# Retention attention and a Snake MLP in one kernel: state sums on VectorE, separate PSUM banks, and a lagged product

## The chip, the cores and the metric

The kernel runs on 1 core of one Trainium2 chip. The metric is device time in microseconds (us). The core has TensorE (PE; its weight loads are shown apart as PEld), VectorE (DVE), ScalarE (ACT), GpSimd (POOL) and SyncE (SP, which here only issues DMAs). Each engine works through its own instructions in order and waits for others by semaphores.

## What is computed

Eight batches of causal attention without softmax, each with 8 heads, 576 tokens and 64 dimensions, with a decay per head; the outputs of all heads are laid side by side and go through an MLP (512 to 2048 to 512) with the Snake activation:

```python
scores = scale * (q @ k.T)                     # per batch and head
ret    = scores * gamma[h] ** (i - j)          # for j <= i, else 0
x      = ret @ v                               # 4608 tokens x 512
h      = x @ w_in
g      = h + sin(alpha * h) ** 2 / (alpha + 1e-9)
out    = g @ w_out
```

## The kernel before, in words

**Attention.** The decay is folded into q and k: `cast` (L121) multiplies the float32 rows by a factor per token and writes float16. A batch has 576 tokens, taken as part 0 (tokens 0 to 255), part 1 (256 to 511) and a small part 2 (the last 64). A part has two chunks of 128 tokens, 0 and 1, or 2 and 3. For each part:

- `transposes` (L155) turns k and q on PE into PSUM (`tr`); `take` (L183) copies them to SBUF (`T`).
- `scores` (L232) multiplies them, in two calls (y = 0, 1) of two head groups each, and masks the result on DVE into `ret`. `scores_small` (L256) does it for part 2. "Mask (p, y)" below is this DVE instruction.
- `outer` (L192) forms the sum of k times v of each chunk (`kv` in PSUM) and copies it on ACT to SBUF (`kvs`). With `spare=True` it uses two banks of the tag `hp`, else two of `mm`.
- `chain` (L218) on POOL: sum n becomes sum n plus the decayed sum n-1 (L223, L224), and the state n, two decayed copies in float16, is made from it (L225).
- `values` (L275) multiplies `ret` with v; `add_states` (L296) adds the part that comes from earlier chunks through the states (part 0 needs state 0, part 1 states 1 and 2, part 2 state 3), and one ACT copy puts the result into `xT` (L311, L316), the input of the MLP.

**The MLP** takes blocks of 512 tokens, nine in all. `gemm1` (L325) computes one of 16 units of a block (128 columns of the hidden layer, 4 matmuls of 128x512) and issues the Sin on ACT; `square` (L341) squares it on a given engine; `product` (L350) on DVE adds the square over alpha to the PSUM value and writes `gT`. Only `product` gives a unit's PSUM bank free. `gemm2` (L361) multiplies `gT` with `w_out` in 16 units, four per output tile; after each fourth one, ACT copies the tile out (`osb`) and SP stores it.

**PSUM** has eight banks: the tag `mm` has two buffers of two banks (transposes, scores, values), `hp` three of one, `op` one. A buffer is waited for until all that used it before is done.

**Order.** Nothing is scheduled automatically: the order in which the code issues instructions is the order on each engine (L384 on). First comes the attention of batch 0, parts 0 and 1, one step after the other (L395 to L426), then alpha's transposition (L427 to L431). The weights come through POOL's DMA queue: `load_w_in` in two halves, `load_w_out` in four groups. On SP, the small DMA `gate` (L434) reads a piece of w_out and so holds the loads behind it back until that group has landed. Then:

- Block 0 (L438 to L446), software-pipelined by hand: gemm1 of unit u, square of u-1 (DVE, ACT and POOL in turn), product of u-2. Units 1 and 2 of every four share one two-bank `mm` tile, `wide`; the others take `hp`.
- gemm2 of block 0, units 0 to 11 (L465), with part 2 of batch 0 and parts 0 and 1 of batch 1 hung on its units by the table `todo` (L450).
- The rest of batch 1's part 1 (L469 to L476).
- Blocks 1 to 8 (L479 on): per unit gemm1 of block n, attention steps of a later batch by the table `todo`, square, product, and gemm2 of block n-1. In block 1 the squares of odd units are on ACT, and the rest of gemm2 of block 0 is done.

Of the kernel before, what the change touches and what calls it, by code (L numbers as in the profile page):

```python
# [9 lines left out]
F32 = mybir.dt.float32  # L10
F16 = mybir.dt.float16
ADD = mybir.AluOpType.add
# [4 lines left out]
def kernel(  # L17
# [128 lines left out]
    class Attention:  # L146
        def __init__(self, b):
            self.b = b
            self.c0 = b * S
            self.T = {}  # L150
            self.ret = {}
            self.state = work.tile([P, 4, 4, 2, D], F16, tag="s16", bufs=2, name="s16")
            self.kvs = work.tile([P, 4, 4, D], F32, tag="kvs", bufs=1, name="kvs")

# [37 lines left out]
        def outer(self, ps, spare=False):  # L192
            if spare:
                kv = [psum.tile([P, 512], F32, tag="hp", bufs=3, name="kv") for g in range(2)]
            else:
                kv2 = psum.tile([P, 2, 512], F32, tag="mm", bufs=2, name="kv")
                kv = [kv2[:, g] for g in range(2)]
            todo = [(x, a, r) for x in range(len(ps)) for a in range(4) for r in range(2)]
            for n, (x, a, r) in enumerate(todo):
                for t in range(2):  # L200
                    for g in range(2):
                        nc.tensor.matmul(  # L202
                            kv[g][halves(t), 256 * x + 64 * a : 256 * x + 64 * a + 64],
                            half[self.b, "k", ps[x]][halves(g), head_of(a, t), r, :],
                            half[self.b, "v", ps[x]][halves(g), head_of(a, t), r, :],
                            start=(n == 0), stop=(n == len(todo) - 1), skip_group_check=True,
                        )
            N = len(ps)
            if spare:
                for g in range(2):  # L210
                    nc.scalar.copy(self.kvs[:, 2 * ps[0] + g], kv[g][:, 0:256].rearrange("p (a d) -> p a d", a=4))
            else:
                nc.scalar.copy(  # L213
                    self.kvs[:, 2 * ps[0] : 2 * ps[0] + 2 * N].rearrange("p (x g) a d -> p g x (a d)", g=2),
                    kv2[:, :, 0 : 256 * N].rearrange("p g (x y) -> p g x y", x=N),
                )

        def chain(self, chunks):  # L218
            kvs = self.kvs
            for n in chunks:  # L220
                if n > 0:
                    s32 = work.tile([P, 4, D], F32, tag="s32", bufs=2, name="s32")
                    nc.gpsimd.tensor_tensor(s32, kvs[:, n - 1], g1.unsqueeze(2).to_broadcast([P, 4, D]), MULT)  # L223
                    nc.gpsimd.tensor_tensor(kvs[:, n], s32, kvs[:, n], ADD)  # L224
                nc.gpsimd.tensor_tensor(  # L225
                    self.state[:, n],
                    kvs[:, n].unsqueeze(2).to_broadcast([P, 4, 2, D]),
                    g2.unsqueeze(3).to_broadcast([P, 4, 2, D]),
                    MULT,
                )  # L230

        def scores(self, p, y):  # L232
            sc = psum.tile([P, 2, 512], F32, tag="mm", bufs=2, name="sc")
            T = self.T[p]
            for z in range(2):
                a = 2 * y + z
                for r in range(2):
                    for t in range(2):
                        for g in range(2):
                            x = 256 * z + 128 * r  # L240
                            nc.tensor.matmul(  # L241
                                sc[halves(g), t, x : x + 128],
                                T[halves(t), g, 0, 128 * a + 64 * r : 128 * a + 64 * r + 64],
                                T[halves(t), g, 1, 128 * a : 128 * a + 128],
                                start=(z == 0 and r == 0), stop=(z == 1 and r == 1), skip_group_check=True,
                            )
            ret = work.tile([P, 2, 512], F16, tag="ret", bufs=4, name="ret")
            nc.vector.tensor_tensor(  # L248
                ret.rearrange("p t (z x) -> p (t z) x", z=2),
                sc.rearrange("p t (z x) -> p (t z) x", z=2),  # L250
                mask[:, 0:256].unsqueeze(1).to_broadcast([P, 4, 256]),
                MULT,
            )
            self.ret[p, y] = ret
# [70 lines left out]
    def gemm1(n, fc, o=None):  # L325
# [4 lines left out]
        for a in range(KT):  # L330
# [1 line left out]
                hps, w_in16[:, a, fc * P : (fc + 1) * P], xT[:, a, bs0 : bs0 + 512],  # L332
                start=(a == 0), stop=(a == KT - 1),
            )
        s_t = work.tile([P, 512], F16, tag="s", bufs=3, name="s_t")
        nc.scalar.activation(  # L336
            s_t, hps, mybir.ActivationFunctionType.Sin, bias=0.0, scale=alpha_t[:, fc : fc + 1],
        )
# [1 line left out]

    def square(n, fc, eng):  # L341
        hps, s_t = hps_of[n, fc]
        ss_t = work.tile([P, 512], F16, tag="ss", bufs=3, name="ss_t")
        if eng is nc.scalar:
            nc.scalar.activation(ss_t, s_t, mybir.ActivationFunctionType.Square)  # L345
        else:
# [36 lines left out]

    with tc.manual_schedule():  # L384
        nc.scalar.dma_start(cn, cn_dram.ap())
        loads(0, (0, 1))
        nc.scalar.dma_start(ident, ident_dram.ap())
        nc.scalar.dma_start(mask, mask_dram.ap())
        nc.scalar.dma_start(alpha_r, moe_alpha.rearrange("(a p) -> a p", p=P))
# [6 lines left out]
        cast(0, "k", 0, V)  # L396
        A.transposes(0, "k")
        A.take(0, "k", A_)
        cast(0, "q", 0, V)
        A.transposes(0, "q")  # L400
        A.take(0, "q", A_)
        cast(0, "v", 0, G_)
        load_w_in(0)
        A.scores(0, 0)
        A.outer((0,), spare=True)
        A.chain((0, 1))
        load_w_in(1)
        cast(0, "k", 1, V)
        A.scores(0, 1)
        A.transposes(1, "k")  # L410
        A.take(1, "k", A_)
        cast(0, "q", 1, V)
        A.transposes(1, "q")
        cast(0, "v", 1, A_)
        A.take(1, "q", A_)
        A.values(0)
        A.add_states(0)
        A.outer((1,), spare=True)
        A.chain((2,))
        for g in range(4):  # L420
            load_w_out(g)
        A.chain((3,))
        A.scores(1, 0)
        A.scores(1, 1)
        A.values(1)
        A.add_states(1)  # L426
        al_ps = psum.tile([P, FC], F32, tag="hp", bufs=3, name="al_ps")  # L427
        nc.tensor.matmul(al_ps, alpha_r, eye, start=True, stop=True, is_transpose=True)
        nc.scalar.copy(alpha_t, al_ps)
        nc.vector.tensor_scalar_add(inva, al_ps, 1e-9)  # L430
        nc.vector.reciprocal(inva, inva)  # L431
# [17 lines left out]
        todo = {  # L449
            0: [lambda: cast(0, "k", 2, V), lambda: cast(0, "q", 2, V), lambda: cast(0, "v", 2, G_)],  # L450
            2: [lambda: cast(1, "k", 0, V)],
            3: [lambda: A.transposes(0, "k"), lambda: A.take(0, "k", A_), lambda: cast(1, "q", 0, V),
                lambda: loads(1, (2,))],
            4: [lambda: A0.transposes(2), lambda: A0.take(2, "k", V), lambda: A0.take(2, "q", V)],
            5: [lambda: A.transposes(0, "q"), lambda: A.take(0, "q", A_), lambda: cast(1, "v", 0, G_),
                lambda: load(2, "k", 0)],
            6: [lambda: A0.scores_small(), lambda: cast(1, "k", 1, V)],
            7: [lambda: A.scores(0, 0), lambda: A.outer((0,)), lambda: A.chain((0, 1)), lambda: load(2, "q", 0)],
            8: [lambda: A.scores(0, 1), lambda: cast(1, "q", 1, V), lambda: load(2, "v", 0)],
            9: [lambda: A0.values(2), lambda: A0.add_states(2)],  # L460
            10: [lambda: A.transposes(1), lambda: A.take(1, "k", A_), lambda: cast(1, "v", 1, A_),
                 lambda: A.take(1, "q", A_), lambda: load(2, "k", 1)],
            11: [lambda: A.values(0), lambda: A.add_states(0), lambda: load(2, "q", 1)],
        }
        for u in range(12):  # L465
            gemm2(0, u, "hp")
# [113 lines left out]
```

## Time and profile before

| | us |
|---|---|
| median of 3 runs | 347.95 (347.75 to 348.88) |
| the profiled execution | 347.28 |
| its span (first to last instruction) | 345.5 |
| PE busy | 311.0 (90%) |
| DVE busy | 243.6 (71%) |
| ACT busy | 180.4 (52%) |
| POOL busy | 152.7 (44%) |
| first gemm1 of block 0 | at 25.57 |
| first gemm1 of block 1 | at 70.32 |

A profile line of the timeline gives the start, the duration, the engine, the source line, the operation with its tiles and shapes, and in brackets how long the engine idled before and what released it. Busy times overlap between engines; a busy PE is not PE at its peak. PEclk is the granted TensorE clock: 1.00 is full.

### The profile page before, as it was taken

How to read it: one execution, taken by the hardware profiler on the slowest of the kernel's cores; microseconds unless marked ns; L12 is line 12 of the kernel's file. 1: busy time of each engine (PE TensorE's matmuls, PEld its weight loads, DVE VectorE, ACT ScalarE, POOL GpSimd, SP SyncE). 2: the span in 40 equal slices, each digit the busy share in tenths (PEclk: the TensorE clock that was granted, in tenths of full speed). 3: DMA queues.
4: the chain of work that ended last, by engine and by line, in shares of the span. 5: the costliest groups of instructions: out<-in, count | busy, mean ns of one | idle time of the engine just before them, and what ended most of it. 6: DMA issues, size and time to landing. Idle time of an engine off the chain costs nothing.

```text
span 345.5 us, 9540 instructions
## 1 busy us (share of the span) xinstructions
PE 311.0 (90%) x4097; PEld 152.5 (44%) x4097; DVE 243.6 (71%) x345; ACT 180.4 (52%) x268; POOL 152.7 (44%) x155
## 2 busy tenths in 40 slices
PE   0378879688899999999999999999999999999994
PEld 0253334434444454445454445544454444444441
DVE  2734686549889998899589858985895666666600
ACT  2345733567685555555555656555555445444511
POOL 0994323565596994598069707960810000000000
PEclk9999999879999999999999999999999999999998
DMA  8999697968724931982298129712111111211142
GB/s 212 256 146 200 122 299 209 236 160 243 163 45 120 251 101 30 260 200 49 46 265 193 35 62 267 194 34 46 33 33 30 32 31 30 58 35 30 31 89 65
DMA packets 72683, 42.72 MB, mean 124 GB/s; under 512 B 15664, under 2 KB 67008, under 8 KB 72640
## 3 DMA queue, kind: packets, MB, share of 16 engines
q1 hardware_dynamic: 68880, 37.78, 44.2%
q0 software_dynamic: 3264, 4.20, 7.4%
q8 instruction: 32, 0.52, 0.6%
q10 hardware_dynamic: 496, 0.13, 0.2%
q14 instruction: 11, 0.09, 0.1%
HBM read 36.83 MB, written 9.44 MB: 134 GB/s over the span
## 4 chain that ended last, share of the span: by engine, by line
PE 75%; DVE 11%; ACT 6%; POOL 3%; issue 2%; DMA 2%; SPq 0%; ACTq 0%; POOLq 0%; DVEq 0%
PE ops L367 32%; PE hps L331 32%; DVE ret L248 3%; PE tr L178 3%; PE o L303 2%; PE o L291 2%; PE sc L241 2%; DVE gT L352 2%; DVE k L133 2%; ACT T L188 2%; DMA q<-in_q_dram 2%; DVE ss_t L347 1%; ACT s_t L336 1%; PE kv L202 1%; DVE q L133 1%
## 5 line engine op out<-in xcount | busy, mean ns | idle before, releaser
L336 ACT ACTIVATE s_t<-hps,alpha_t 128x512 f16<-128x512 f32 x144 | 98.7, 687 | 109.8 <-PE hps L331 108.1
L331 PE MATMUL hps<-xT,w_in 128*128 128x512 f16 x576 | 149.1, 386 | 7.3 <-ACT s_t L336 3.5
L367 PE MATMUL ops<-w_out,gT 128*128 128x512 f16 x576 | 145.1, 380 | 0.0
L352 DVE SCALAR_TENSOR_TENSOR gT<-ss_t,inva,hps 128x512 f16<-128x512 f16 x144 | 107.1, 747 | 11.9 <-ACT ss_t L345 6.7
L347 DVE TENSOR_TENSOR ss_t<-s_t 128x512 f16<-128x512 f16 x126 | 77.0, 611 | 37.6 <-ACT s_t L336 37.5
L331 PEld LDWEIGHTS <-w_in 128*128 128x128 f16 x576 | 56.5, 99 | 76.1 <-issue 12.8
L367 PEld LDWEIGHTS <-gT 128*128 128x128 f16 x576 | 52.7, 98 | 58.2 <-DVE gT L352 0.3
L225 POOL TENSOR_TENSOR s<-kvs,cn 128x512 f16<-128x512 f32 x32 | 36.3, 1135 | 66.1 <-ACT kvs L213 64.2
L248 DVE TENSOR_TENSOR ret<-sc,mask 128x1024 f16<-128x1024 f32 x32 | 38.1, 1218 | 12.5 <-PE sc L241 12.5
L373 ACT COPY osb<-ops 128x512 f32<-128x512 f32 x36 | 21.1, 586 | 19.1 <-PE ops L367 17.4
L188 ACT COPY T<-tr 128x1024 f16<-128x1024 f16 (+1 forms) x28 | 23.1, 829 | 15.0 <-PE tr L178 13.6
L133 POOL TENSOR_TENSOR q<-q,cn 128x1024 f16<-128x1024 f32 x12 | 23.9, 1988 | 0.0
L224 POOL TENSOR_TENSOR kvs<-s,kvs 128x256 f32<-128x256 f32 x24 | 17.4, 724 | 9.6 <-ACT kvs L213 4.1
L311 ACT CAST xT<-o 128x1024 f16<-128x1024 f32 x16 | 16.2, 1014 | 9.9 <-PE o L303 9.9
L133 POOL TENSOR_TENSOR k<-k,cn 128x1024 f16<-128x1024 f32 x10 | 20.2, 2023 | 0.0
L137 POOL CAST v<-v 128x1024 f16<-128x1024 f32 x12 | 14.4, 1197 | 10.8 <-DMA v<-in_v_dram 10.8
L190 DVE COPY T<-tr 128x1024 f16<-128x1024 f16 (+1 forms) x20 | 10.5, 529 | 11.7 <-ACT T L188 11.0
L178 PE MATMUL tr<-ident,k 64*64 64x64 f16 x512 | 7.5, 201 | 11.9 <-DVE k L133 11.9
L223 POOL TENSOR_TENSOR s<-kvs,cn 128x256 f32<-128x256 f32 x24 | 18.0, 752 | 0.0
L241 PE MATMUL sc<-T 64*64 64x128 f16 x512 | 12.3, 230 | 4.5 <-ACT T L188 2.2
L241 PEld LDWEIGHTS <-T 64*64 64x64 f16 x512 | 9.3, 113 | 10.9 <-issue 10.7
L178 PEld LDWEIGHTS <-k 64*64 64x64 f16 x512 | 5.7, 114 | 18.0 <-DVE k L133 12.5
(45 smaller groups left out, 151.0 us busy)
## 6 DMA issues: line engine op xcount, KB each, us to landing
out_dram<-osb SPq DMA_DIRECT2D x72, 128.0 KB, 2.3
k<-in_k_dram SPq DMA_DIRECT2D x16, 512.0 KB, 5.1
q<-in_q_dram SPq DMA_DIRECT2D x16, 512.0 KB, 5.8
v<-in_v_dram SPq DMA_DIRECT2D x16, 512.0 KB, 6.8
w_in<-in_moe_w_in_dram POOLq DMA_DIRECT2D x8, 256.0 KB, 7.0
w_out<-in_moe_w_out_dram POOLq DMA_DIRECT2D x4, 512.0 KB, 10.2
ks<-in_k_dram SPq DMA_DIRECT2D x16, 64.0 KB, 3.8
qs<-in_q_dram SPq DMA_DIRECT2D x16, 64.0 KB, 3.4
```

Of the source, the lines that this page charges most:

```text
L133: eng.tensor_tensor(d_, s_, f_, MULT)
L178: nc.tensor.matmul(tr[halves(t), g, col : col + 64], x_, ident[halves(g), :], start=(n == 0), stop=(n == len(todo) - 1), is_transpose=True ...
L188: eng.copy(self.T[p][:, :, w, :], s_)
L225: nc.gpsimd.tensor_tensor(self.state[:, n], kvs[:, n].unsqueeze(2).to_broadcast([P, 4, 2, D]), g2.unsqueeze(3).to_broadcast([P, 4, 2, D]), ...
L241: nc.tensor.matmul(sc[halves(g), t, x : x + 128], T[halves(t), g, 0, 128 * a + 64 * r : 128 * a + 64 * r + 64], T[halves(t), g, 1, 128 * a ...
L248: nc.vector.tensor_tensor(ret.rearrange("p t (z x) -> p (t z) x", z=2), sc.rearrange("p t (z x) -> p (t z) x", z=2), mask[:, 0:256].unsque ...
L331: nc.tensor.matmul(hps, w_in16[:, a, fc * P : (fc + 1) * P], xT[:, a, bs0 : bs0 + 512], start=(a == 0), stop=(a == KT - 1),)
L336: nc.scalar.activation(s_t, hps, mybir.ActivationFunctionType.Sin, bias=0.0, scale=alpha_t[:, fc : fc + 1],)
L347: eng.tensor_tensor(ss_t, s_t, s_t, MULT)
L352: nc.vector.scalar_tensor_tensor(gT[n][:, fc, :], ss_t, inva[:, fc : fc + 1], hps, MULT, ADD)
L367: nc.tensor.matmul(o, gT[n][:, fk, c * P : (c + 1) * P], w_out16[:, fk, :], start=(fk == 0), stop=(fk == FC - 1),)
L373: nc.scalar.copy(osb, o)
```

## The change

- Each unit of block 0 gets a bank of its own out of six: even units `hp`, odd ones in turn one half of an `mm` buffer, another, and `op`.
- In batch 0, and in part 1 of batch 1, the chunk sums aren't copied to SBUF and added by POOL. `sum_in_place` copies only sum 0 on ACT and adds the others on DVE, straight from PSUM, in four instructions of 128x64 per chunk; POOL keeps the states (`to_state`).
- `scores` is split into its PE part and its mask, so that a cast can go between them.
- alpha's transposition moves up between the transposes of k and q; the loads of batch 0's last 64 tokens go right behind its other loads; the gate waits for w_out group 1 instead of 2; the second half of w_in is issued behind the states 0 and 1.
- Part 2 of batch 0 moves from gemm2 of block 0 into block 0; the table `todo` of gemm2 is rearranged accordingly, with values (0) at unit 10.
- The squares of block 0 are shared out anew (7 on DVE, 6 on ACT, 3 on POOL; before 6, 5 and 5), and the buffers `s` and `ss` go from 3 to 4.
- In block 1 the product lags by one unit: it is issued behind the next unit's square, and the last one in block 2.

```diff
             if spare:
-                for g in range(2):
-                    nc.scalar.copy(self.kvs[:, 2 * ps[0] + g], kv[g][:, 0:256].rearrange("p (a d) -> p a d", a=4))
+                self.kv = kv
...
+        def sum_in_place(self, p):
+            kv = [self.kv[g][:, 0:256].rearrange("p (a d) -> p a d", a=4) for g in range(2)]
+            if p == 0:
+                nc.scalar.copy(self.kvs[:, 0], kv[0])
+            for c in range(max(1, 2 * p), 2 * p + 2):
+                for a in range(4):
+                    nc.vector.scalar_tensor_tensor(
+                        self.kvs[:, c, a], self.kvs[:, c - 1, a], g1[:, a : a + 1], kv[c % 2][:, a], MULT, ADD
+                    )
+
+        def to_state(self, n):
+            nc.gpsimd.tensor_tensor(
+                self.state[:, n],
+                self.kvs[:, n].unsqueeze(2).to_broadcast([P, 4, 2, D]),
+                g2.unsqueeze(3).to_broadcast([P, 4, 2, D]),
+                MULT,
+            )
...
-        s_t = work.tile([P, 512], F16, tag="s", bufs=3, name="s_t")
+        s_t = work.tile([P, 512], F16, tag="s", bufs=4, name="s_t")
...
-        ss_t = work.tile([P, 512], F16, tag="ss", bufs=3, name="ss_t")
+        ss_t = work.tile([P, 512], F16, tag="ss", bufs=4, name="ss_t")
...
-        loads(0, (0, 1))
+        loads(0, (0, 1, 2))
...
         A.take(0, "k", A_)
+        al_ps = psum.tile([P, FC], F32, tag="hp", bufs=3, name="al_ps")
+        nc.tensor.matmul(al_ps, alpha_r, eye, start=True, stop=True, is_transpose=True)
         cast(0, "q", 0, V)
         A.transposes(0, "q")
         A.take(0, "q", A_)
+        nc.scalar.copy(alpha_t, al_ps)
+        nc.vector.tensor_scalar_add(inva, al_ps, 1e-9)
+        nc.vector.reciprocal(inva, inva)
         cast(0, "v", 0, G_)
         load_w_in(0)
-        A.scores(0, 0)
+        A.scores_pe(0, 0)
+        cast(0, "k", 1, V)
+        A.scores_mask(0, 0)
         A.outer((0,), spare=True)
-        A.chain((0, 1))
-        load_w_in(1)
-        cast(0, "k", 1, V)
-        A.scores(0, 1)
+        A.scores_pe(0, 1)
         A.transposes(1, "k")
         A.take(1, "k", A_)
         cast(0, "q", 1, V)
+        A.sum_in_place(0)
+        A.to_state(0)
+        A.to_state(1)
+        load_w_in(1)
+        A.scores_mask(0, 1)
...
         A.outer((1,), spare=True)
-        A.chain((2,))
+        A.scores_pe(1, 0)
+        A.scores_mask(1, 0)
+        A.sum_in_place(1)
+        A.to_state(2)
         for g in range(4):
             load_w_out(g)
-        A.chain((3,))
-        A.scores(1, 0)
+        A.to_state(3)
         A.scores(1, 1)
...
-        nc.sync.dma_start(gate, w_out16[:, 8, 0:64])
-        loads(0, (2,))
-        loads(1, (0, 1))
-        wide = None
+        nc.sync.dma_start(gate, w_out16[:, 4, 0:64])
+        loads(1, (0, 1, 2))
+        todo = {
+            3: [lambda: cast(0, "k", 2, V), lambda: cast(0, "q", 2, G_), lambda: cast(0, "v", 2, G_)],
+            5: [lambda: A.transposes(2), lambda: A.take(2, "k", V), lambda: A.take(2, "q", V)],
+            8: [lambda: A.scores_small()],
+            11: [lambda: A.values(2), lambda: A.add_states(2)],
+        }
         for u in range(18):
             if u < 16:
-                if u % 4 == 1:
-                    wide = psum.tile([P, 2, 512], F32, tag="mm", bufs=2, name="hps")
-                gemm1(0, u, wide[:, u % 4 - 1] if u % 4 in (1, 2) else None)
+                if u % 2 == 0:
+                    o = None
+                elif u % 6 == 5:
+                    o = psum.tile([P, 512], F32, tag="op", bufs=1, name="hps")
+                else:
+                    o = psum.tile([P, 2, 512], F32, tag="mm", bufs=2, name="hps")[:, 0]
+                gemm1(0, u, o)
+            for f in todo.get(u, []):
+                f()
             if u >= 1 and u < 17:
-                square(0, u - 1, [V, A_, G_][(u - 1) % 3])
+                square(0, u - 1, G_ if u % 5 == 0 else A_ if u % 2 else V)
...
         todo = {
...
+            0: [lambda: cast(1, "k", 0, V)],
+            2: [lambda: A.transposes(0, "k"), lambda: A.take(0, "k", A_), lambda: cast(1, "q", 0, V)],
+            4: [lambda: A.transposes(0, "q"), lambda: A.take(0, "q", A_), lambda: cast(1, "v", 0, G_),
                 lambda: load(2, "k", 0)],
...
+            5: [lambda: cast(1, "k", 1, V)],
+            6: [lambda: A.scores(0, 0), lambda: A.outer((0,)), lambda: A.chain((0, 1)), lambda: load(2, "q", 0)],
+            7: [lambda: A.scores(0, 1), lambda: cast(1, "q", 1, V), lambda: load(2, "v", 0)],
+            9: [lambda: A.transposes(1), lambda: A.take(1, "k", A_), lambda: cast(1, "v", 1, A_),
+                lambda: A.take(1, "q", A_), lambda: load(2, "k", 1)],
+            10: [lambda: A.values(0), lambda: A.add_states(0), lambda: load(2, "q", 1)],
         }
...
         A.outer((1,), spare=True)
-        A.chain((2, 3))
+        A.sum_in_place(1)
+        A.to_state(2)
         A.scores(1, 1)
         A.values(1)
         A.add_states(1)
+        A.to_state(3)
...
-                if n < NBLK:
-                    square(n, u, A_ if n == 1 and u % 2 == 1 else V)
+                if n == 1:
+                    square(n, u, A_ if u % 2 == 1 else V)
+                    if u > 0:
+                        product(n, u - 1)
+                elif n < NBLK:
+                    if n == 2 and u == 0:
+                        product(1, 15)
+                    square(n, u, V)
                     product(n, u)
```

More of the change, by code (lines that the diff above doesn't have):

```diff
@@ L151, in __init__ @@
             self.ret = {}
+            self.sc = {}
             self.state = work.tile([P, 4, 4, 2, D], F16, tag="s16", bufs=2, name="s16")
@@ L224, in chain, with scores_pe @@
                     nc.gpsimd.tensor_tensor(kvs[:, n], s32, kvs[:, n], ADD)
[L225 to L230, printed above, removed]
+                self.to_state(n)
         def scores(self, p, y):
+            self.scores_pe(p, y)
+            self.scores_mask(p, y)
+        def scores_pe(self, p, y):
             sc = psum.tile([P, 2, 512], F32, tag="mm", bufs=2, name="sc")
@@ L246, in scores, with scores_mask @@
                             )
+            self.sc[p, y] = sc
+        def scores_mask(self, p, y):
+            sc = self.sc.pop((p, y))
             ret = work.tile([P, 2, 512], F16, tag="ret", bufs=4, name="ret")
@@ L426 @@
         A.add_states(1)
[L427 to L431, printed above, removed]
-        gate = work.tile([P, 64], F16, tag="gate", bufs=1, name="gate")
-        nc.sync.dma_start(gate, w_out16[:, 8, 0:64])
-        loads(0, (2,))
-        loads(1, (0, 1))
-        wide = None
+        gate = work.tile([P, 64], F16, tag="gate", bufs=1, name="gate")
+        nc.sync.dma_start(gate, w_out16[:, 4, 0:64])
[6 more added lines that the diff above has]
+        }
         for u in range(18):
             if u < 16:
-                if u % 4 == 1:
-                    wide = psum.tile([P, 2, 512], F32, tag="mm", bufs=2, name="hps")
-                gemm1(0, u, wide[:, u % 4 - 1] if u % 4 in (1, 2) else None)
+                if u % 2 == 0:
[7 more added lines that the diff above has]
+                f()
             if u >= 1 and u < 17:
-                square(0, u - 1, [V, A_, G_][(u - 1) % 3])
+                square(0, u - 1, G_ if u % 5 == 0 else A_ if u % 2 else V)
             if u >= 2:
@@ L449 @@
         todo = {
[L450 to L455, printed above, removed]
-                lambda: load(2, "k", 0)],
[L457 to L463, printed above, removed]
+            0: [lambda: cast(1, "k", 0, V)],
+            2: [lambda: A.transposes(0, "k"), lambda: A.take(0, "k", A_), lambda: cast(1, "q", 0, V)],
+            4: [lambda: A.transposes(0, "q"), lambda: A.take(0, "q", A_), lambda: cast(1, "v", 0, G_),
+                lambda: load(2, "k", 0)],
+            5: [lambda: cast(1, "k", 1, V)],
[4 more added lines that the diff above has]
+            10: [lambda: A.values(0), lambda: A.add_states(0), lambda: load(2, "q", 1)],
         }
```

## The prediction

> **What bounds the kernel now.** I read the 40 slices first (the PE row is filled from the twelfth slice on), then the busy times by stage. Columns: stretch; its length; busy time and count of PE, PEld, DVE, ACT, POOL; granted clock; DMA share; GB/s.
>
> ```profile
> 0.00:25.57 25.57, 9.57 (x334) 7.68 (x335) 11.15 (x9) 9.76 (x14) 16.24 (x24) 1.00 0.97 205
> 25.57:48.80 23.23, 19.75 (x80) 8.08 (x79) 14.69 (x26) 13.11 (x22) 8.51 (x10) 1.00 0.99 196
> 48.80:70.32 21.52, 15.09 (x401) 8.55 (x402) 13.06 (x13) 9.98 (x14) 9.79 (x10) 0.91 0.90 239
> 70.32:102.00 31.68, 28.56 (x488) 13.42 (x487) 25.13 (x32) 23.72 (x40) 20.38 (x21) 0.95 0.58 145
> ...
> 129.00:156.00 27.00, 27.00 (x423) 13.30 (x422) 23.09 (x34) 15.10 (x24) 18.69 (x19) 1.00 0.65 159
> ```
>
> From 129 us on PE has no gap, so what is won or lost before 102 us goes to the end one to one. The four stretches are: attention of batch 0; gemm1 of block 0; gemm2 of block 0 with attention of batch 1; block 1. No engine is full in the first three: order and waits bound them. So I went on to the timelines (start, duration, engine, line, what; in brackets the idle time before and who ended it).
>
> ```profile
> 29.92 3.61 PE L331 MATMUL hps<-xT,w_in 128*128 128x512 f16 x16 [0.78 <-ACT s_t L336]
> ...
> 34.30 3.61 PE L331 MATMUL hps<-xT,w_in 128*128 128x512 f16 x16 [0.78 <-ACT s_t L336]
> ...
> 38.99 3.61 PE L331 MATMUL hps<-xT,w_in 128*128 128x512 f16 x16 [1.07 <-ACT s_t L336]
> ...
> 43.44 1.89 PE L331 MATMUL hps<-xT,w_in 128*128 128x512 f16 x8 [0.84 <-ACT s_t L336]
> ```
>
> Block 0: units 2, 6, 10 and 14 write the second half of the tile `wide`, and each starts when the Sin that reads the first half ends. That is 3.47 us.
>
> ```profile
> 12.15 2.79 DVE L133 TENSOR_TENSOR k<-k,cn 128x1024 f16<-128x1024 f32 x1
> ...
> 20.45 2.36 DVE L248 TENSOR_TENSOR ret<-sc,mask 128x1024 f16<-128x1024 f32 x2 [3.15 <-PE sc L241]
> ...
> 48.89 2.05 DVE L133 TENSOR_TENSOR k<-k,cn 128x1024 f16<-128x1024 f32 x1
> ...
> 50.99 0.45 PE L178 MATMUL tr<-ident,k 64*64 64x64 f16 x32 [2.22 <-DVE k L133]
> ```
>
> A cast takes 1.22 alone and 2.05 to 2.79 when POOL works beside it. The two masks of part 1 run back to back, 20.45 to 22.81; from there values, states, the xT copy and gemm1 at 25.57 follow in a chain (2.76 us).
>
> ```profile
> 77.35 1.02 PE L331 MATMUL hps<-xT,w_in 128*128 128x512 f16 x4 [0.48 <-DVE gT L352]
> ...
> 83.97 1.02 PE L331 MATMUL hps<-xT,w_in 128*128 128x512 f16 x4 [0.39 <-DVE gT L352]
> ```
>
> Block 1: PE waits for a product, because a unit needs the bank that the product three units back frees (`hp` has 3).
>
> **Part 1, attention of batch 0.** The casts: k1 lands at 10.9 (issue 3.42 plus 7.5). Its cast now comes ahead of mask (0,0), and POOL's chain is no longer beside it: 10.95 to 12.18, not to 14.94. mask (0,0) ends at 13.3; the transposes of k1 need its banks: 13.4 to 14.0; take to 15.06; behind it on ScalarE the copy of sum 0 (0.38) to 15.4. The first four added state sums wait for that copy, and on VectorE mask (0,1) is queued behind them.
>
> The sums, 128x64 from PSUM, are in no row. Nearest: 128x512 of the same operation, 0.75, two in a row 1.40, so 0.65 from start to start; less 448 elements at 1.04 ns (the masks: 1.22 at 1024 elements, 0.42 at 256) leaves 0.18 start to start and 0.28 alone. A 128x16 TENSOR_SCALAR took 0.17, its successor began 0.21 after it. Ends 0.15 and 0.28; I take 0.19, between the two nearest. The Trainium skill (VectorE: DVE Perf Modes, Side-by-side: where the cycles go) counts some 158 cycles besides the elements; worked out from that page, an estimate of 0.23 each, and eight would be 1.85, not 1.5.
>
> Four end at 16.2, mask (0,1) at 17.4, and values (0) starts at 17.45 (17.80 before). Mask (1,0) then ends at 21.3 (21.6). But eight sums (1.5) now stand ahead of mask (1,1): it ends at 24.05, not 22.81. State 2 is ready by 23.2, so it is not late. With the 2.76 us of chain gemm1 starts at 26.85: **+1.3** (ends +0.9 and +2.0). The removed copies and POOL additions pay nothing here: they ran beside the masks.
>
> alpha: alpha_r and eye land by 7.8, and 0.28 of PE fits ahead of the q transposes at 8.56; hidden under the wait for k1. SP's six small loads (0.39 MB, 1.3 us at 290 GB/s) go ahead of w_in, whose first half landed by 20.4 and is wanted at 26.9: nothing. The second half is issued at 17.5 (18.1), w_out at 23.1 (23.1): nothing.
>
> **Part 2, block 0.** Walked unit by unit: the first two units run slow (3.5 us, as at 25.57), the others 0.87 each, and the work of part 2 of batch 0 adds 1.1 on PE. One new wait: unit 9 needs a bank of the small scores, so their mask on VectorE (0.6). PE ends 17.1 us after its start (19.6 before). VectorE has 16 products (0.65) and 7 squares (0.37), a cast, two takes, one mask: 14.3, so it is close behind; ScalarE 13.5. The last square of POOL (1.04) still holds products 14 and 15, which end 20.1 us after the start, not 22.7: **-2.6**. Ends: -3.5 (all four stalls) and 0 (VectorE sets the pace of 1.12 per unit that it has now). The fourth buffers of s and ss take away a wait of 0.66 (35.43); it is in this walk.
>
> **Part 3, to block 1.** The casts ks and qs are gone from the head of VectorE's queue (48.22 to 48.89): **-0.67**. The v cast on POOL, landed earlier, falls beside products, which read PSUM and keep their 0.75; the k cast takes 1.22, not 2.05: **-0.83** (ends 0 and -0.83). The gate waits for w_out group 1 (landed 32.9), not 2 (36.1), and the small loads are no longer between: the loads of batch 1 start 7 us earlier on SP. They were not late, so this pays nothing. Groups 2 and 3 of w_out now share the DMA engines: wanted at 45.7 and 48.5, landed at 36.1 and 38.7. If all 3.1 MB went first (10.7 us) they would cost 1 us; I take 0.
>
> From the k transposes to the end of the q1 cast took 9.99 us; without the small transposes, scores, mask (0.42) and takes (0.49), and with k1 cast earlier, 9.0: **-1.0** (ends -1.4 and 0). Then as in part 1: eight sums ahead of mask (1,1), 1.5, less 0.2 for the xT copy that now goes ahead of the osb copy: **+1.3** (ends +0.7 and +2.2).
>
> Block 1 so starts 1.3 - 2.6 - 0.67 - 0.83 - 1.0 + 1.3 = **-2.5** us, at 67.8.
>
> **Part 4, block 1.** The product of unit u now stands behind the square and the attention work of unit u+1 on VectorE, and gemm1 of unit u+3 waits for it. In today's times: unit 4 needs product 1; that now follows square 2, so Sin 2 (ends 77.05): 77.05 + 0.42 + 0.75 = 78.2, 0.9 late. Take, k1 cast and square 4 move by as much (square 4: 84.0), then product 3 ends at 84.75 and frees unit 6, which began at 81.22. With the 2.3 us of PE work between, unit 7 starts at 86.9, not 83.97: 2.9 late. Behind it PE idled 0.18, 0.83 and 0.62, which takes up 1.63: **+1.27**. Other end: the waits of products for ScalarE's squares (0.94 and 0.76) go and no bank is late, -1.7; upper end +2.9, nothing taken up.
>
> A clock drop is not in this sum. Rows: the clock was 0.57 in 66.0 to 70.3 and eight matmuls at 70.32 took 3.42 (1.89 at 43.44); the idle 2.22 before 50.99 left the next 32 transposes at 0.45, undisturbed. The Trainium skill (TensorE: Matmul & The Clock Gate, Part 1) has the clock halved after an idle window of about 3.4 us: by that rule the new idle of 2.3 before unit 6 costs nothing. By the first row it could cost 3.42 - 1.73 = 1.7 us.
>
> **Sum.** -2.5 + 1.27 = -1.23. The profiled execution took 347.28 (span 345.5 and 1.78 around it), so 346.05 there; the median of the runs shown is 347.95, 0.67 above, so **346.7**.
>
> **Rivals.** (a) The lag is free: block 1 keeps its pace or gains, -2.5 to -4.2, at 344.6. For it: VectorE's two waits for ACT squares. Against: four bank waits of PE, that lag lengthens. (b) Slower: products held back behind masks starve gemm1 of its three banks. Price +2.9, and 1.7 if the clock falls: -2.5 + 4.6 = +2.1, 350.1. It decides once units 6 to 9 start over 2.5 us late and nothing is taken up. For it: VectorE busy 25.13 of 31.68. (c) The change doesn't do what it says: block 0 stays at VectorE's and ScalarE's pace, so only 0.4 of 2.6 is won: +1.0, 348.9.
>
> **Chances.** Forecast 0.42, from 345.6 to 347.9; (a) 0.22; (b) 0.21; (c) 0.15. About 0.3% (1.04 us) is what a measurement here can tell from no change. Faster: 0.62 of the forecast and all of (a), 0.48. Slower: (b) and half of (c), 0.29. Within: 0.23. The likeliest case's own range with the sums' ends is 345.0 to 348.4; to leave out 2 in 10 it must reach into (a) and (b): 343.7 to 350.2.
>
> **What would show it.** gemm1 of block 0 later, near 26.9, with small sums between the last masks; no waits of L331 for ACT's s_t in block 0; its last product near 47; first k transposes near 48; gemm1 of block 1 near 67.8; then longer waits of PE for gT at its units 4 and 6, and unit 15 near +32.3 instead of +30.85. Wrong if the sums take over 0.3 each, if block 0 keeps 1.12 per unit, or if block 1 shows no longer waits.

## The result and the profile after

The changed kernel takes 351.2 us (median of 11 runs, 350.58 to 352.34) beside 347.75 for the kernel before (11 runs, 346.24 to 350.26): a ratio of 1.0096 [1.0067, 1.0124], slower by some 3.3 us. The forecast was 346.7. The profiled execution took 350.85, its span is 349.1.

First the same stretches as before, by stage (stretch; length; busy time and count of PE, PEld, DVE, ACT, POOL; granted clock; DMA share; GB/s):

```profile
0.00:25.57 25.57, 9.81 (x333) 8.01 (x334) 12.30 (x23) 7.91 (x11) 11.86 (x20) 1.00 1.05 226
25.57:48.80 23.23, 20.34 (x144) 8.60 (x143) 16.48 (x29) 14.45 (x24) 6.68 (x8) 1.00 1.14 240
48.80:70.32 21.52, 16.56 (x365) 8.93 (x350) 11.07 (x16) 8.99 (x11) 10.26 (x9) 0.89 0.76 197
70.32:102.00 31.68, 25.74 (x464) 12.29 (x462) 21.10 (x30) 21.51 (x36) 14.82 (x15) 0.91 0.49 123
...
129.00:156.00 27.00, 27.00 (x404) 13.27 (x393) 23.12 (x33) 14.70 (x21) 18.69 (x20) 1.00 0.59 148
```

The edges are those of the kernel before, so each stretch now holds some work of its neighbours. What can be read off is that PE did more in the second and third (20.34 and 16.56 us, before 19.75 and 15.09) and less in the fourth (25.74 against 28.56). PE was kept waiting in block 1. The last row is as full as it was; what is lost before it reaches the end.

The timelines give the stages by their own marks. Attention of batch 0:

```profile
10.86 1.22 DVE L133 TENSOR_TENSOR k<-k,cn 128x1024 f16<-128x1024 f32 x1
...
20.96 1.61 DVE L224 SCALAR_TENSOR_TENSOR kvs<-kvs,cn,kv 128x64 f32<-128x64 f32 x8
22.49 1.22 DVE L269 TENSOR_TENSOR ret<-sc,mask 128x1024 f16<-128x1024 f32 x1
...
26.47 4.00 PE L352 MATMUL hps<-xT,w_in 128*128 128x512 f16 x9 [1.10 <-ACT xT L332]
```

The early cast of k1 takes 1.22 instead of 2.79. Then eight sums stand ahead of mask (1,1) (22.49), and gemm1 starts at 26.47 instead of 25.57. Block 0, and the way to block 1:

```profile
37.86 2.75 PE L352 MATMUL hps<-xT,w_in 128*128 128x512 f16 x12 [0.53 <-DVE rets L288]
...
47.27 1.21 DVE L133 TENSOR_TENSOR k<-k,cn 128x1024 f16<-128x1024 f32 x1
...
48.53 0.45 PE L179 MATMUL tr<-ident,k 64*64 64x64 f16 x32 [1.47 <-DVE k L133]
...
62.96 1.61 DVE L224 SCALAR_TENSOR_TENSOR kvs<-kvs,cn,kv 128x64 f32<-128x64 f32 x8
64.49 1.22 DVE L269 TENSOR_TENSOR ret<-sc,mask 128x1024 f16<-128x1024 f32 x1
...
68.47 3.57 PE L352 MATMUL hps<-xT,w_in 128*128 128x512 f16 x8 [1.10 <-ACT xT L332]
```

PE's waits for Sin of 0.78 to 1.07 are gone from block 0; the one for the small mask (0.53) has come. The k cast is down from 2.05 to 1.21. Block 1 starts at 68.47 instead of 70.32: up to here the change has won 1.85 us. Then block 1:

```profile
76.58 1.02 PE L352 MATMUL hps<-xT,w_in 128*128 128x512 f16 x4 [1.30 <-DVE gT L373]
...
79.96 1.21 DVE L133 TENSOR_TENSOR k<-k,cn 128x1024 f16<-128x1024 f32 x1
81.09 1.26 DVE L368 TENSOR_TENSOR ss_t<-s_t 128x512 f16<-128x512 f16 x1
82.28 0.73 DVE L373 SCALAR_TENSOR_TENSOR gT<-ss_t,inva,hps 128x512 f16<-128x512 f16 x1
...
83.07 1.87 PE L352 MATMUL hps<-xT,w_in 128*128 128x512 f16 x4 [2.55 <-DVE gT L373]
...
86.55 1.03 PE L352 MATMUL hps<-xT,w_in 128*128 128x512 f16 x4
...
96.52 1.02 PE L352 MATMUL hps<-xT,w_in 128*128 128x512 f16 x4 [0.37 <-DVE gT L373]
...
98.31 1.02 PE L352 MATMUL hps<-xT,w_in 128*128 128x512 f16 x4 [0.52 <-DVE gT L373]
...
104.09 1.02 PE L352 MATMUL hps<-xT,w_in 128*128 128x512 f16 x4 [0.35 <-DVE gT L373]
```

Unit 6 (83.07) waits 2.55 us for product 3 (82.28), which stands on VectorE behind the cast of k1 and square 4. Its four matmuls then take 1.87 instead of 1.02. Unit 7 follows at 86.55, and units 12, 13 and the first of block 2 wait once more. The clock around that wait (columns as above):

```profile
79.60:83.07 3.47, 0.42 (x17) 0.35 (x16) 3.47 (x5) 1.34 (x3) 2.50 (x3) 0.93 0.20 48
...
83.00:84.90 1.90, 1.83 (x8) 0.45 (x10) 1.80 (x3) 0.00 (x0) 1.82 (x3) 0.50 0.77 231
...
86.50:90.00 3.50, 3.31 (x58) 1.71 (x57) 2.33 (x5) 2.26 (x5) 2.00 (x4) 1.00 0.60 165
```

It stands at 0.50 just when PE has work again (in finer windows from 82.55 to 85.96), and is back at 1.00 by 86.50. The start of block 2 before:

```profile
101.17 1.03 PE L331 MATMUL hps<-xT,w_in 128*128 128x512 f16 x4
```

From its first gemm1 to that of block 2, block 1 takes 35.62 us (68.47 to 104.09), before 30.85 (70.32 to 101.17): 4.77 more. So block 2 starts 2.92 later, and the last store ends 3.6 later.

### The profile page after: what moved, and what is told of

It reads as the page before. It is cut to its first block, busy times and chain, and to the rows that moved or that the text cites. A ratio compares the mean times of both kernels' runs of the same rounds, so it can differ in the third digit from the quotient of the medians.

```text
span 349.1 us, 9530 instructions
## 1 busy us (share of the span) xinstructions
PE 313.1 (90%) x4097; PEld 153.7 (44%) x4097; DVE 241.5 (69%) x365; ACT 178.9 (51%) x264; POOL 142.5 (41%) x144
## 4 chain that ended last, share of the span: by engine, by line
PE 74%; DVE 11%; ACT 6%; DMA 5%; issue 2%; POOL 1%; ACTq 0%; POOLq 0%
PE hps L352 31%; PE ops L388 31%; DMA k<-in_k_dram 4%; DVE ret L269 3%; DVE gT L373 3%; PE o L312 3%; PE o L324 3%; PE tr L179 3%; ACT T L189 2%; PE sc L258 2%; DVE ss_t L368 2%; ACT s_t L357 1%; PE kv L203 1%; DVE kvs L224 1%; ACT ss_t L366 1%
## 5 line engine op out<-in xcount | busy, mean ns | idle before, releaser
L368 DVE TENSOR_TENSOR ss_t<-s_t 128x512 f16<-128x512 f16 x127 | 74.6, 587 | 47.4 <-ACT s_t L357 47.3
L229 POOL TENSOR_TENSOR s<-kvs,cn 128x512 f16<-128x512 f32 x32 | 35.3, 1106 | 81.6 <-ACT kvs L213 70.2
L312 PE MATMUL o<-ret,v 64*64 64x128 f16 x512 | 11.6, 232 | 6.8 <-DVE ret L269 5.3
L242 POOL TENSOR_TENSOR kvs<-s,kvs 128x256 f32<-128x256 f32 x19 | 13.8, 726 | 7.7 <-ACT kvs L213 6.3
L312 PEld LDWEIGHTS <-v 64*64 64x64 f16 x512 | 9.0, 115 | 11.0 <-issue 11.0
```

Of the source, the lines that this page charges most:

```text
L229: nc.gpsimd.tensor_tensor(self.state[:, n], self.kvs[:, n].unsqueeze(2).to_broadcast([P, 4, 2, D]), g2.unsqueeze(3).to_broadcast([P, 4, 2, ...
L312: nc.tensor.matmul(self.o[halves(t), g, N * a : N * a + N], x, y, start=(n == 0), stop=False, skip_group_check=True,)
L368: eng.tensor_tensor(ss_t, s_t, s_t, MULT)
```

## The experiments

**My theory** after this profile: parts 1 to 3 of the change gain, and the lag in block 1 alone makes the kernel slower. Two rivals: block 1 is late because of what comes ahead of it, the state in which the rearranged stages leave the engines, and not because of the lag; or the lag's waits would be made good again, and it is the clock drop that makes them dear. The runs lie in two groups, e1 to e4 on one chip and e5 to e8 on another; each ratio is to the kernel before in the same group (medians 347.29 and 346.56; 347.75 beside the change). So runs of different groups are compared by their ratios.

### e1: the change without the lag

```diff
-                if n == 1:
-                    square(n, u, A_ if u % 2 == 1 else V)
-                    if u > 0:
-                        product(n, u - 1)
-                elif n < NBLK:
-                    if n == 2 and u == 0:
-                        product(1, 15)
-                    square(n, u, V)
+                if n < NBLK:
+                    square(n, u, A_ if n == 1 and u % 2 == 1 else V)
                     product(n, u)
```

> The changed kernel with the product of block 1 back in its own unit, everything else of the change kept. Theory A (the loss is the lag, which holds products behind masks and casts so that gemm1 waits for its three banks): block 1 takes 30.9 us from its first gemm1 to block 2's first, as before, not 35.6; block 1 still starts at 68.5, 1.85 us ahead of the kernel before; so 346.0, that is 0.993 to 0.996 of before. Rival B (the loss in block 1 comes from the other moves: POOL's casts, the loads or the ScalarE copies falling differently there): block 1 stays near 35 us and the time near 351.

Measured: 345.58, ratio 0.9949 [0.9924, 0.9974]. PE in block 1, from its first unit over units 6 and 7 to block 2:

```profile
69.53 3.57 PE L352 MATMUL hps<-xT,w_in 128*128 128x512 f16 x8 [1.10 <-ACT xT L332]
...
80.59 1.04 PE L352 MATMUL hps<-xT,w_in 128*128 128x512 f16 x4
...
83.33 1.02 PE L352 MATMUL hps<-xT,w_in 128*128 128x512 f16 x4 [0.39 <-DVE gT L373]
...
100.53 1.03 PE L352 MATMUL hps<-xT,w_in 128*128 128x512 f16 x4
```

Block 1 takes 31.00 us (before 30.85), its waits are those of before, and unit 6 runs at full clock. (The loads landed about 1 us later in this execution, so stretches are to be compared, not moments.) The rest of the change is a gain of 1.8 us, and the lag turned it into a loss: from 0.9949 to 1.0096 is a factor of 1.0148, 5.1 us.

### e2: the kernel before with the lag alone

The edit of e1 the other way round, on the kernel before.

> The kernel before with only the lag added to block 1. Theory A: +3.5 to +4.8 us, 351.2 to 352.5, first gemm1 of block 1 unchanged at 70.3, a wait of PE for gT of 2 us or more ahead of its unit 6, and a halved clock behind it. Rival B: no more than 1 us of change. Rival C (the lag hurts only together with the freed POOL and earlier casts): between the two, under +2.5.

Measured: 352.6, ratio 1.0143 [1.0099, 1.0186], +5.0 us. Units 4, 6 and 7 of block 1:

```profile
78.58 1.02 PE L331 MATMUL hps<-xT,w_in 128*128 128x512 f16 x4 [1.41 <-DVE gT L352]
...
85.07 1.87 PE L331 MATMUL hps<-xT,w_in 128*128 128x512 f16 x4 [2.55 <-DVE gT L352]
...
89.11 1.89 PE L331 MATMUL hps<-xT,w_in 128*128 128x512 f16 x4
```

The same waits, to 0.11 us, with the order of the kernel before in front of them, and the clock falls here too: to 0.50 from 84.0 to 90.8, twice as long as in the change, so unit 7 is slow as well (1.89) and block 1 takes 36.47 us (70.60 to 107.07). The time lies just above the expected range. This rules out the first rival: the lag costs 5 us by itself, with the old order ahead of it as with the new one.

### e3: PE kept busy in the wait

The change with 18 matmuls of 128x256 ahead of unit 6, into a half of a PSUM bank that nobody reads. They change nothing of the output.

```diff
+        def keep_busy(self, count):
+            for i in range(count):
+                nc.tensor.matmul(
+                    self.kv2[:, i % 2, 256:512], w_in16[:, 0, 0:128], w_in16[:, 1, 0:256], start=True, stop=True,
+                )
...
-                at_unit(5, lambda: A.scores(0, 0), lambda: cast(2, "q", 1, G_))
+                at_unit(5, lambda: A.scores(0, 0), lambda: A.keep_busy(18), lambda: cast(2, "q", 1, G_))
```

> The changed kernel (lag kept) with 18 matmuls of 128x256 added on PE in the wait ahead of unit 6 of block 1, into columns that nothing reads: extra work, output unchanged. Of the 4.8 us that block 1 lost, theory A1 gives about 1.5 to the clock that falls to 0.50 behind that wait: 349.7, clock 1.00 behind the wait, unit 7 of block 1 1.5 us sooner after the block's start. Theory A2 (the waits are all of it; the slow matmuls are hidden under VectorE's backlog): 351.2, no change, though the clock stays at 1.00.

Measured: 349.99, ratio 1.0073 [1.0045, 1.0102]. The added matmuls, then units 6, 7 and 8:

```profile
79.21 2.12 PE L230 MATMUL kv<-w_in 128*128 128x256 f16 x18
...
81.81 1.02 PE L358 MATMUL hps<-xT,w_in 128*128 128x512 f16 x4 [0.48 <-DVE gT L379]
...
83.99 1.03 PE L358 MATMUL hps<-xT,w_in 128*128 128x512 f16 x4
...
86.36 1.02 PE L358 MATMUL hps<-xT,w_in 128*128 128x512 f16 x4 [0.93 <-DVE gT L379]
```

VectorE ahead of unit 8 (mask (0,1), square 6, products 5 and 6):

```profile
83.47 1.21 DVE L275 TENSOR_TENSOR ret<-sc,mask 128x1024 f16<-128x1024 f32 x1
...
84.61 1.03 DVE L374 TENSOR_TENSOR ss_t<-s_t 128x512 f16<-128x512 f16 x1
...
85.57 1.39 DVE L379 SCALAR_TENSOR_TENSOR gT<-ss_t,inva,hps 128x512 f16<-128x512 f16 x2
```

The clock stays at 1.00 (78.5 to 86.0). Unit 6 starts nearly as late as in the change (+14.34 us after the block's start, there +14.60), but runs in 1.02, and unit 7 comes at +16.52 instead of +18.08. Of these 1.56 us, 0.26 lie ahead of unit 6, where the matmuls added can have done nothing: in this execution the slow matmuls at the start of the block ended sooner. The other 1.30 are the clock. Of them unit 8 gives 0.75 back, waiting 0.93 instead of 0.18 for its own bank (product 5, behind mask (0,1) and square 6). Block 1 takes 34.72, 0.90 less than in the change, 0.64 of it behind the start of unit 6.

So the second rival holds for a small part only. By this trace the half clock behind unit 6 is 0.64 of the 4.77 us. At full clock block 1 with the lag still takes 3.87 us more than before (34.72 against 30.85). The times don't settle it: by the ratios the added matmuls gain 0.8 us, but the two intervals overlap.

### e4: no lag, and the last four sums behind the mask

On e1: the four sums of chunk 3 and its state are issued behind mask (1,1), in both batches.

```diff
-        A.sum_in_place(1)
+        A.sum_in_place(1, (2,))
         A.to_state(2)
         for g in range(4):
             load_w_out(g)
+        A.scores(1, 1)
+        A.sum_in_place(1, (3,))
         A.to_state(3)
-        A.scores(1, 1)
...
-        A.sum_in_place(1)
+        A.sum_in_place(1, (2,))
         A.to_state(2)
         A.scores(1, 1)
+        A.sum_in_place(1, (3,))
```

> As the first run of this call (no lag), and in both attention parts the mask (1,1) goes ahead of the last four state sums, so four sums instead of eight stand before it. If the sums are on the path that starts gemm1, each place gains 0.8 us: first gemm1 of block 0 at 25.65 and of block 1 1.6 us sooner than without the edit, about 344.4. If something else is as late (state 2 from POOL, the copies), the gain is under 0.4 in all.

Measured: 343.63, ratio 0.9894 [0.9855, 0.9932], some 1.9 us below e1. The four sums that stay, the mask, and the first gemm1 of blocks 0 and 1:

```profile
20.89 0.85 DVE L224 SCALAR_TENSOR_TENSOR kvs<-kvs,cn,kv 128x64 f32<-128x64 f32 x4
21.66 1.22 DVE L269 TENSOR_TENSOR ret<-sc,mask 128x1024 f16<-128x1024 f32 x1
...
25.63 4.63 PE L352 MATMUL hps<-xT,w_in 128*128 128x512 f16 x11 [1.10 <-ACT xT L332]
...
66.44 3.57 PE L352 MATMUL hps<-xT,w_in 128*128 128x512 f16 x8 [1.10 <-ACT xT L332]
```

Four sums fewer ahead of the mask (0.8 us) are 0.84 us at block 0 (25.63; 26.47 in the change, whose order is the same up to there but for this). What the sums delay is the mask, and through it the chain to gemm1.

### e5: half of the lag

The change with the order turned: the product of the last unit ahead of this unit's square, not behind it.

```diff
                 if n == 1:
-                    square(n, u, A_ if u % 2 == 1 else V)
                     if u > 0:
                         product(n, u - 1)
+                    square(n, u, A_ if u % 2 == 1 else V)
```

> The changed kernel with the lag kept, but the product of unit u-1 issued ahead of the square of unit u, still behind the attention work of unit u. This tells the two things apart behind which the lag puts a product. If the square (with its wait for the Sin, and 1.26 us under POOL's work in unit 4) is what counts, the wait of 2.55 us ahead of unit 6 falls to about 1.3, the clock stays up, and block 1 takes about 32.5 us: 348. If the attention work counts (take, k1 cast, masks), the wait stays over 2 us and the time near 351.

Measured: 347.57, ratio 1.0018 [0.9995, 1.0041]. Units 6 and 13 of block 1, and block 2:

```profile
80.79 1.02 PE L352 MATMUL hps<-xT,w_in 128*128 128x512 f16 x4 [1.37 <-DVE gT L373]
...
95.52 1.02 PE L352 MATMUL hps<-xT,w_in 128*128 128x512 f16 x4 [1.40 <-DVE gT L373]
...
100.79 1.03 PE L352 MATMUL hps<-xT,w_in 128*128 128x512 f16 x4
```

The wait at unit 6 is 1.37 instead of 2.55, the unit runs in 1.02, and block 1 takes 32.51 (68.28 to 100.79). The cost of the lag is graded: 31.00 without it, 32.51 behind the attention work alone, 35.62 behind that and the square.

### e6: no lag, and the sums back on POOL

On e1: `outer` copies `kv` on ACT again, and POOL's `chain` replaces `sum_in_place`; the rest of the new order stays.

```diff
-                self.kv = kv
+                for g in range(2):
+                    nc.scalar.copy(self.kvs[:, 2 * ps[0] + g], kv[g][:, 0:256].rearrange("p (a d) -> p a d", a=4))
...
-        A.sum_in_place(0)
-        A.to_state(0)
-        A.to_state(1)
+        A.chain((0, 1))
...
-        A.sum_in_place(1)
-        A.to_state(2)
+        A.chain((2,))
```

> No lag, and the state sums back on POOL with both copies on ScalarE, as before the change; all else of the change kept. If the sums on VectorE only cost (theory A: 1.3 us at each of the two places ahead of mask (1,1), and 0.9 of waiting ahead of mask (0,1)), first gemm1 of block 0 starts 24.3 to 24.8 against 26.5, block 1 near 66.3, and the time is 342 to 343.5, under the run with the mask first (343.6). Rival: POOL's chain inflates the casts again (1.22 to 2 us or more) or its state 2 comes after mask (1,1), and the time is 345.5 or more, no better than the sums on VectorE.

Measured: 341.51, ratio 0.9845 [0.9817, 0.9873]. The cast of q1 beside POOL's chain, the two masks of part 1, state 2, and gemm1 of blocks 0 and 1:

```profile
13.15 1.74 DVE L133 TENSOR_TENSOR q<-q,cn 128x1024 f16<-128x1024 f32 x1
...
18.75 2.35 DVE L270 TENSOR_TENSOR ret<-sc,mask 128x1024 f16<-128x1024 f32 x2 [2.72 <-PE sc L259]
...
21.19 1.04 POOL L230 TENSOR_TENSOR s<-kvs,cn 128x512 f16<-128x512 f32 x1
...
23.99 3.57 PE L353 MATMUL hps<-xT,w_in 128*128 128x512 f16 x8 [1.10 <-ACT xT L333]
...
63.45 1.89 PE L353 MATMUL hps<-xT,w_in 128*128 128x512 f16 x8 [1.10 <-ACT xT L333]
```

In the new order POOL's sums are not late: the masks run back to back from 18.75, and gemm1 starts at 23.99, 1.58 sooner than in the kernel before and 2.48 sooner than in the change. POOL beside VectorE still stretches a cast (1.74), but gemm1 is not seen to suffer. Against e1 the sums on VectorE cost 3.6 us by the ratios. That is more than expected: both starts are sooner, and the time lies below the expected range. In the profiled execution, the fastest of the six, part of this is the clock: its mean granted clock was 1.00 (the other five 0.979 to 0.989), and the first eight matmuls of block 1 took 1.89 instead of 3.57 without any help.

### e7: the six banks alone

On the kernel before: only the assignment of PSUM banks in block 0.

```diff
-                if u % 4 == 1:
-                    wide = psum.tile([P, 2, 512], F32, tag="mm", bufs=2, name="hps")
-                gemm1(0, u, wide[:, u % 4 - 1] if u % 4 in (1, 2) else None)
+                if u % 2 == 0:
+                    o = None
+                elif u % 6 == 5:
+                    o = psum.tile([P, 512], F32, tag="op", bufs=1, name="hps")
+                else:
+                    o = psum.tile([P, 2, 512], F32, tag="mm", bufs=2, name="hps")[:, 0]
+                gemm1(0, u, o)
```

> The kernel before with one edit: block 0 on six separate banks. If the banks are the gain of block 0, the four waits for ACT's s_t go and block 0 is 1.5 to 2.6 us shorter: 345.2 to 346.3. If VectorE and ScalarE set its pace, under 0.6 us: 347 or more.

Measured: 343.23, ratio 0.9907 [0.9873, 0.9940], a gain of 3.2 us by one small edit, more than the 1.5 to 2.6 expected of block 0. gemm1 of block 0 and of block 1:

```profile
25.49 15.66 PE L331 MATMUL hps<-xT,w_in 128*128 128x512 f16 x64 [0.89 <-ACT xT L311]
...
65.01 3.57 PE L331 MATMUL hps<-xT,w_in 128*128 128x512 f16 x8 [1.10 <-ACT xT L311]
```

All 64 matmuls of block 0 run without a gap in 15.66 us. From the start of block 0 to that of block 1 it is 39.52 us; 44.75 before, 42.00 in the change, 39.46 in e6. Of the 5.23 less than before, 4.08 are there at the last product of block 0, and 0.84 is the k cast behind it, which takes 1.21 here too, because it now comes ahead of POOL's v cast and not beside it. The trace shows more than the times: the profiled execution of e7 is its fastest (342.2), and that of the kernel before (347.28) is above the median of this group. e6 has part 2 of batch 0 inside block 0 and the other loads and casts, e7 has not: all that together wins nothing in this stretch.

### e8: e6, and PE kept warm

e6 with five matmuls of 128x512 into an unread bank ahead of block 0 and nine ahead of block 1, where PE waits for the last mask and the xT copy. They change nothing of the output.

```diff
+    def keep_busy(count):
+        idle = psum.tile([P, 512], F32, tag="hp", bufs=3, name="idle")
+        for i in range(count):
+            nc.tensor.matmul(idle, w_in16[:, 0, 0:128], w_in16[:, 1, 0:512], start=True, stop=True)
...
-        A.values(1)
+        A.values(1, lambda: keep_busy(3))
         A.add_states(1)
+        keep_busy(2)
```

> As the second run of this call, with matmuls that nothing needs put into PE's waits ahead of the first gemm1 of block 0 (3 and 2) and of block 1 (4 and 5), so that PE does not go idle there; the output is unchanged. Each of these blocks begins with 8 matmuls at half rate, 3.4 to 3.6 us instead of 1.9. If the fillers keep the clock up at both, 3 us less than without them; if at block 1 alone, about 1.5 less; if the waits are too short to matter or the fillers come late, no gain or up to 0.5 us lost.

Measured: 339.62, ratio 0.9798 [0.9764, 0.9831], the best version found, 6.9 us under the kernel before in its group. The added matmuls ahead of block 0, then its first units:

```profile
20.70 1.46 PE L352 MATMUL idle<-w_in 128*128 128x512 f16 x3
...
23.50 0.94 PE L352 MATMUL idle<-w_in 128*128 128x512 f16 x2
24.80 5.34 PE L360 MATMUL hps<-xT,w_in 128*128 128x512 f16 x24 [0.37 <-ACT xT L335]
```

gemm1 starts 0.8 later than in e6, but its first 24 matmuls take 5.34 instead of 7.08. The gain on e6 is 1.9 us between the medians of one group; the two intervals overlap, but five of the six executions are faster than all six of e6. The two traces don't show this gain. Of the 0.74 us won by the end of block 0's gemm1, 0.63 goes again at the k cast, which now falls beside POOL and takes 1.84 instead of 1.21, and the profiled execution of e6 needed no help at block 1. The mean granted clock of the executions differs, though: 0.979 to 0.989 in five of the six of e6, 0.994 to 1.00 in e8. So the matmuls may well keep the clock up where e6 mostly loses it; that this is the 1.9 us was not shown.

## Why the prediction was wrong, step by step

**The failed step is Part 4**, the lag: forecast +1.27, measured +4.77. Its mechanism and its beginning were right. Unit 4 was to be 0.9 late and is 1.08 late; unit 6 was to start 14.43 after the block's start (84.75 less 70.32) and started at 14.60. What failed is what comes behind: the recovery, the last units, and the clock. e3, with the lag but at full clock behind unit 6, tells them apart:

- **The recovery was set too high.** In e3 unit 7 is 2.87 late (+16.52, before +13.65), as forecast (2.9). Of this 1.63 was to be taken up by the short waits behind it. Only 0.51 was, by unit 11 (25.40 after the block's start, before 23.04), because the lag makes unit 8 wait too, 0.93 for product 5. That is 1.12 more than forecast.
- **The walk stopped at unit 9**, but the lag applies to units 9 to 15 as well. Products 9 and 10 stand behind the masks (1,0) and (1,1) of batch 2 (at 94.07 and 96.39 on VectorE in the change), units 12 and 13 wait for them, and block 2 waits 0.35 for product 13: 1.5 lost again between unit 11 and block 2, in e3 as in the change.
- **The clock was left out**, 0.90: 0.64 behind unit 6, and 0.26 in the slow start of the block. In the change unit 7 is 4.43 late (+18.08), 1.30 of it by the clock behind unit 6, but half of that disappears in waits that e3 has in its place. The prediction had a price for the clock, 1.7, and kept it out of the sum because a wait of 2.22 before 50.99 had left the clock alone. But that one wait was not all that counted: from 79.60 to 83.07 PE did 0.42 us of work, in an idle 0.51, some score matmuls, and an idle 2.55. The Trainium skill (TensorE: Matmul & The Clock Gate, Part 1) puts the drop to half after an idle window of about 3.4 us. Here no wholly idle window of that length came before the drop: it came at 82.55, 2.0 us after the end of the score matmuls, and the measurement decides. Read with the wait alone, as the prediction did, the rule promised no cost.

Together 1.27 + 1.12 + 1.5 + 0.90 is the 4.77 that was measured (to 0.02).

A slip in the list of signs: "unit 15 near +32.3 instead of +30.85" gives the start of block 2 as that of unit 15, which was at +29.58 before. As block 2's start, +32.3 is near the walk's own 30.85 + 1.27, so it was no check of the units behind 9.

Rival (b) is what happened, with the mechanism named: products held back behind masks, three banks, the clock on top. Its condition, units over 2.5 us late and nothing taken up, held in sum: the block's end is later than unit 7 by 0.34. Its price, 2.9 and 1.7, was 4.6 for a measured 4.77, but that it came so near is luck: the parts measured are 3.87 for the waits and 0.90 for the clock. It had 0.21. Its piece of evidence, though, was no good: VectorE's share. From unit 7 to block 2 VectorE was busy 12.87 of 17.54 us in the change and 15.11 of 17.20 in e1. The lag made it idler and the block longer. What had to be read was the time a bank is held, to the end of its product.

**Part 1**, forecast +1.3: +0.9, the lower end. The sums were sized well (1.61 for eight, 0.20 each; forecast 0.19). The frame was too narrow: the new order was compared with the old kernel's, in which the cast of k1 ran beside POOL's chain (2.79 us). The chain starts no later there (12.77, in e6 12.72); what is won is the cast of k1 ahead of it (1.23). In the new order with POOL's sums (e6) the stage takes 1.58 less than before, so the sums on VectorE cost 2.48 there, not 0.9. The reordering was a gain that the sums used up.

**Part 2**, forecast -2.6: -1.85 (20.87 from the first gemm1 to the last product, before 22.72). The stalls went, the wait for the small mask came (0.53 for a forecast of 0.6). "The first two units run slow" failed: the first twelve matmuls do, 0.43 apart, not eight. The banks alone (e7) win 5.2 us to block 1 in the trace, 3.2 in the times; rival (c) is ruled out. The change makes less of them (42.00 against 39.52). Part 2 of batch 0 is not the reason, since e6 has it too and takes 39.46; e6 lacks the sums on VectorE, and 0.66 of what it has over the change is the shorter slow start of block 0 (7.08 against 7.74 for 24 matmuls).

**Part 3**: the casts ks and qs -0.67 (forecast -0.67), the k cast -0.84 (-0.83), transposes to q1 cast -0.65 (-1.0), the last leg with the eight sums +1.26 (+1.3). Block 1 started 1.85 earlier for a forecast 2.5. Part 1 was 0.4 better than forecast; Part 2 (0.75) and the transposes (0.35) were worse.

The miss is 4.5 us between the medians (351.2 against 346.7) and 4.80 for the profiled execution (350.85 against 346.05). Of these 4.80, 3.50 is block 1 and 0.65 the stages ahead of it. Another 0.36 is lost inside block 2, where the `kv` matmuls wait 0.63 for masks instead of 0.27. All three kernels with the whole lag show this (e2 and e3 too, 0.62 and 0.63), and e1 has 0.27 again, so it is the lag's as well. The last 0.29 came at the copy of the last output tile: an idle of 0.32 instead of 0.04, whose cause the trace doesn't show.

## What to carry to other kernels

A software lag lengthens the time that a PSUM bank is held. Before issuing a freeing instruction later, walk every unit with the banks there are, to the last one, and against what stands in that engine's queue; the engine's busy share doesn't show it. When work goes to another engine, price it against the old engine in the new order too, since the reordering may already have removed the reason. And where PE waits ahead of a long run of matmuls, don't price the clock by the longest single wait alone; look at the work around it too. No threshold was found here. A few matmuls that nothing needs can pay there, which the times of e8 suggest.

## What the hardware showed that was not expected

- With 0.42 us of matmuls in the 3.47 us up to the end of the wait the clock fell to 0.50, in the change and in e2, and stayed there for 3.4 us (82.55 to 85.96) and 6.8 us (84.0 to 90.8). With 3.18 busy in 4.00 (e3, 78.5 to 82.5) it stayed at 1.00. The busy time alone doesn't decide it: ahead of block 1 it fell with 1.61 busy in 4.00 in e3 (60.0 to 64.0, 0.95 and 0.50 from then on), and stayed with 1.68 in 3.95 in e6 (59.50 to 63.45).
- Work added to PE can make the kernel faster: e3's 2.12 us of matmuls shortened block 1 by 0.64 from unit 6 on, and with e8's fourteen the median is 1.9 us under e6.
- The granted clock reads 1.00 at the start of block 0 (27.0 to 29.0 in the change), though its first matmuls run 0.43 apart there and 0.22 later. There the row doesn't show the half rate; the spacing does.
- Eight 128x64 sums from PSUM on VectorE took 1.61 us, 0.20 each, four took 0.85.
